# Moving expert 1's weight preparation and expert 0's scalings off VectorE, and ending the last expert on a single tile

## The chip, the cores and the metric

The kernel runs on one core of a Trainium2 chip. The time is device microseconds of one execution; the median of three executions before the change is 903.67 us (902.35 to 905.14). The core's engines are named as the profile names them: PE (TensorE, matrix products), DVE (VectorE), ACT (ScalarE), POOL (GpSimd) and SP (the queue that starts the transfers).

## The reference

An xLSTM-like recurrence (4 batches, 8 heads, 768 steps, head size 40) makes x of shape 3072 x 320. A soft mixture of 8 experts follows, and then the part that the change is about:

```
logits = x @ w_gate ; P = exp(logits - max)
for _ in range(8):
    P /= P.sum(1) + 1e-9 ; P /= P.sum(0) + 1e-9 ; P *= N / E      # Sinkhorn
for e in range(8):
    h = maximum(x @ w1[e], 0) ; out += P[:, e:e+1] * (h @ w2[e])   # F = 1024
```

N is 3072, D 320, F 1024. x here is the output of the soft mixture, of the form c @ slot_out with 32 slots, so x @ w1[e] is one product with 96 rows on the contraction side (three f16 pieces of 32).

## The kernel before

The 3072 rows are 24 tiles of 128 (`acc[:, i, :]` holds the sum of tile i, 128x320 f32). Matrix products run in f16 with each operand split in a high and a low half: h*w is hh*wh + hh*wl + hl*wh. The low half of a weight or of an activation is "value minus high half", so each split costs one cast and one subtraction.

Expert 0 is done in six blocks of four tiles (`g1`, `g2`). Its sums go to `acc` unscaled, since its combine weights are known only after the eight Sinkhorn steps, which run beside it on DVE (`sinkhorn_a`, `sinkhorn_b`, one half of a step after some of the tiles; `SK` lists them). `EXTRA` lists what else is issued after each of those tiles: the maxima of expert 1's w2 (`amax`), its scale (`pow2_w`), its high and low halves (`prep_1`), and the halves of its first-layer operand (`s1_c`). Ps[:, i, e] is the combine weight of tile i and expert e times two scales (`scale_p`, L1157 to L1161).

Experts 1 to 7 go through a planner in slots. A unit is one tile (`One`, 4 slots) or a pair of tiles (`Two`, 7 slots, a Strassen-like scheme with 7 products for 2x2 blocks). Eight triples (One, Two) make an expert: 88 slots. A unit's first-layer products and their ReLUs (`produce`: PE writes z into one of three PSUM banks, ACT and DVE read it) are issued 14 slots ahead of its second-layer products (`consume`). `Two` needs sums of quarters of w2 (`sum_w`, in place in `raw`) and their halves (`sum_h`, `sum_l`). Later expert weights are prepared by ACT and POOL (`prep_s`, `sum_l` with e other than 1) at slots fixed by `plan`. A unit's sums are added to `acc` by `drain`, `drain_x` and `drain_y`; for expert 1 each is preceded by `first` (L1553 to L1555), which multiplies the 128x320 tile of expert 0 by Ps[:, i, 0].

ACT, DVE, POOL and PE work their instructions strictly in the order of issue here (a manual schedule), so whatever stands ahead of an instruction on its engine delays it. A z bank comes free when the last ReLU that reads it is done; PE waits for it there.

Of the kernel before, what the change touches and what calls it, by code (L numbers as in the profile page):

```python
# [20 lines left out]
def mlstm_moe_kernel(  # L21
# [1459 lines left out]

    def quarter(a, b):
        return raw[:, a * KH:(a + 1) * KH, b * DH:(b + 1) * DH]

    SUMS = [((0, 0), (0, 1), (0, 0), ALU.subtract), ((0, 1), (1, 1), (0, 1), ALU.subtract),
            ((1, 1), (0, 0), (1, 1), ALU.subtract), ((1, 0), (1, 0), (1, 1), ALU.add)]

    def sum_w(j):
        o, a, b, op = SUMS[j]
        nc.gpsimd.tensor_tensor(out=quarter(*o), in0=quarter(*a), in1=quarter(*b), op=op)  # L1490

    def sum_h(e, j):
        nc.scalar.activation(
            out=wth[:, e % 2, j], in_=quarter(*SUMS[j][0]), func=AF.Copy, scale=scw[e][1] if e == 1 else 1.0,
        )
# [207 lines left out]
    for tt in range(TPB):  # L1703
        st = (NB - 2) * TPB + tt
        plan(4 * tt + 3, sinkhorn, st)
        for op, kk in EXTRA.get(st, ()):
            plan(4 * tt + 3, op, 1, kk)

    def prep_s(e, kk):
        ks = slice(2 * kk, 2 * kk + 2)  # L1710
        t = src2[e][:, ks, :]
        nc.scalar.activation(out=t, in_=t, func=AF.Copy, scale=scw[e][1])  # L1712
        nc.gpsimd.tensor_tensor(out=wl[e][:, ks, :], in0=t, in1=wh[e][:, ks, :], op=ALU.subtract)  # L1713
# [112 lines left out]
```

## Time and profile before

| | us |
|---|---|
| median of three executions | 903.67 (902.35 to 905.14) |
| the profiled execution | 898.99 |
| its span, first to last instruction | 897.3 |
| PE busy | 862.9 (96%) |
| DVE busy | 716.1 (80%) |
| ACT busy | 558.1 (62%) |
| POOL busy | 588.9 (66%) |

Busy is the time in which an engine had an instruction under way. A row of the timeline reads: start, duration, engine, line, operation, output <- input, shapes; in square brackets stands how long the engine was idle before it and what ended that. Rows with x2 or more are several instructions merged. A row of the waits reads: engine and tile that waited <- what released it: total, times, longest.

### The profile page before, as it was taken

The page shows a single profiled execution, that of the slowest core. Times are in us where ns is not written, and L with a number is a line of the kernel's source. Part 1 is how long each engine was busy: PE and PEld are TensorE (multiplying, and loading weights), DVE is VectorE, ACT ScalarE, POOL GpSimd, SP SyncE. Part 2 cuts the span into 40 slices and gives each one's busy share as a digit, 9 for nine tenths or more (in the row PEclk, how much of TensorE's full clock was granted, in tenths as well). Part 3 has the DMA queues.
Part 4 walks back from the last instruction along what each step waited for, and adds up shares of the span by engine and source line. Part 5 has one row for each costly group of instructions (what it writes and reads, how often), then busy time and mean ns, then how long its engine had stood idle before and what let it go on. Part 6 is the DMA issues. An engine that isn't in the chain of part 4 may idle for free.

```text
span 897.3 us, 26669 instructions
## 1 busy us (share of the span) xinstructions
PE 862.9 (96%) x10996; PEld 728.8 (81%) x10996; DVE 716.1 (80%) x1534; ACT 558.1 (62%) x1110; POOL 588.9 (66%) x596
## 2 busy tenths in 40 slices
PE   7999997899998989999999999999999999999997
PEld 5878884356676878888999899989889998988996
DVE  7777875455899989897788788878987897888774
ACT  7656653353245567668766776687577767767662
POOL 5766660000014679967996799689769977997663
PEclk9999999999999999999999999999999999999999
DMA  8999999960100121204110201051100110000111
GB/s 170 173 199 185 191 248 323 326 182 1 55 6 30 31 57 26 60 2 39 45 60 2 66 16 61 5 64 45 31 5 10 40 31 5 19 1 31 46 46 60
DMA packets 136402, 67.11 MB, mean 75 GB/s; under 512 B 105209, under 2 KB 130041, under 8 KB 136281
## 3 DMA queue, kind: packets, MB, share of 16 engines
q1 hardware_dynamic: 136009, 64.92, 30.1%
q8 instruction: 86, 1.41, 0.7%
q14 instruction: 35, 0.29, 0.2%
q10 hardware_dynamic: 224, 0.30, 0.1%
q0 software_dynamic: 48, 0.20, 0.1%
HBM read 60.17 MB, written 5.02 MB: 73 GB/s over the span
## 4 chain that ended last, share of the span: by engine, by line
PE 66%; DVE 10%; DMA 7%; POOL 7%; issue 5%; ACT 3%; SPq 1%; DVEq 0%; POOLq 0%; ACTq 0%
PE y L1540 15%; PE z L1508 6%; POOL op L1520 3%; DMA bigy<-in_moe_w_dram 3%; PE pss L432 2%; DVE tmr L1517 2%; PE ptk L383 2%; PE oa L477 2%; PE y L1312 2%; PE y L1313 2%; PE y L1314 2%; DMA wa<-in_moe_w_dram 1%; POOL raw L1490 1%; PE pe L402 1%; DVE acc L1560 1%
## 5 line engine op out<-in xcount | busy, mean ns | idle before, releaser
L1520 POOL TENSOR_TENSOR op<-tmr,op 128x512 f16<-128x512 f32 x280 | 319.1, 1168 | 22.1 <-ACT op L1588 19.0
L1635 PEld LDWEIGHTS <-op 128*128 128x128 f16 x4704 | 328.3, 98 | 0.6 <-issue 0.5
L1588 ACT CAST op<-tmr 128x512 f16<-128x512 f32 x280 | 170.0, 616 | 108.1 <-DVE tmr L1517 55.7
L1540 PE MATMUL y<-wx,ch 128*128 128x320 f16 x1344 | 219.0, 299 | 0.0
L1517 DVE SCALAR_TENSOR_TENSOR tmr<-z,tmr 128x512 f32<-128x512 f32 x168 | 114.7, 683 | 56.5 <-ACT op L1514 50.0
L1540 PEld LDWEIGHTS <-ch 128*128 128x128 f16 x1344 | 122.7, 98 | 35.0
L1508 PE MATMUL z<-cst,sst 96*128 96x128 f16 x1344 | 131.0, 219 | 11.7 <-DVE tmr L1517 4.9
L1594 POOL TENSOR_TENSOR tmr<-tmr 128x512 f32<-128x512 f32 x56 | 71.2, 1271 | 95.2 <-ACT tmr L1514 95.2
L1508 PEld LDWEIGHTS <-sst 96*128 96x128 f16 x1344 | 100.2, 98 | 33.6 <-issue 11.3
L1514 ACT ACTIVATE tmr<-z 128x512 f32<-128x512 f32 x112 | 64.8, 596 | 63.5 <-PE z L1508 51.7
L1517 DVE SCALAR_TENSOR_TENSOR ch<-z,ch 128x512 f16<-128x512 f32 x112 | 77.0, 688 | 18.1 <-ACT ch L1514 16.6
L1517 DVE SCALAR_TENSOR_TENSOR op<-z,op 128x512 f16<-128x512 f32 x112 | 76.2, 681 | 0.0
L1514 ACT ACTIVATE ch<-z 128x512 f16<-128x512 f32 x112 | 66.1, 591 | 2.8 <-PE my__8101 L1635 1.3
L1514 ACT ACTIVATE op<-z 128x512 f16<-128x512 f32 x112 | 66.6, 595 | 0.1
L1490 POOL TENSOR_TENSOR raw<-raw 128x640 f32<-128x640 f32 x28 | 43.8, 1565 | 8.3 <-DVE acc L1323 7.3
L1314 PE MATMUL y<-wh,hl 128*128 128x320 f16 x160 | 47.8, 299 | 0.3 <-DVE hl L1295 0.3
L1312 PE MATMUL y<-wh,hh 128*128 128x320 f16 x160 | 47.8, 299 | 0.0
L1313 PE MATMUL y<-wl,hh 128*128 128x320 f16 x160 | 47.8, 299 | 0.0
L411 ACT ACTIVATE dd<-pe 128x512 f32<-128x512 f32 x48 | 29.2, 609 | 29.4 <-PE pe L402 28.9
L1294 ACT ACTIVATE hh<-z 128x512 f16<-128x512 f32 x48 | 26.6, 595 | 33.1 <-PE z L1291 32.8
L1713 POOL TENSOR_TENSOR wx<-raw,wx 128x640 f16<-128x640 f32 x24 | 33.6, 1408 | 15.1 <-ACT raw L1712 15.1
L439 DVE TENSOR_TENSOR dd<-pss,dd 128x512 f32<-128x512 f32 x48 | 31.0, 685 | 14.7 <-PE pss L432 11.9
(1078 smaller groups left out, 1653.0 us busy)
## 6 DMA issues: line engine op xcount, KB each, us to landing
wa<-in_moe_w_dram SPq DMA_DIRECT2D x18, 512.0 KB
raw<-in_moe_w_dram SPq DMA_DIRECT2D x28, 320.0 KB
kq<-in_k_dram SPq DMA_DIRECT2D x24, 160.0 KB
kq<-in_q_dram SPq DMA_DIRECT2D x24, 160.0 KB
vz<-in_v_dram SPq DMA_DIRECT2D x24, 160.0 KB
xr<-in_o_gate_dram SPq DMA_DIRECT2D x24, 160.0 KB
wb<-in_moe_w_dram SPq DMA_DIRECT2D x6, 640.0 KB
out_dram<-acc SPq DMA_DIRECT2D x24, 160.0 KB
```

The lines of the kernel that those rows point to most:

```text
L1312: nc.tensor.matmul(y, hh[:, kc, ts], wh[e][:, kc, :], start=(kc == 0), stop=False)
L1313: nc.tensor.matmul(y, hh[:, kc, ts], wl[e][:, kc, :], start=False, stop=False)
L1314: nc.tensor.matmul(y, hl[:, kc, ts], wh[e][:, kc, :], start=False, stop=(kc == KF - 1))
L1490: nc.gpsimd.tensor_tensor(out=quarter(*o), in0=quarter(*a), in1=quarter(*b), op=op)
L1508: nc.tensor.matmul(z[:, k, :], Sst[e][:, kc * P:(kc + 1) * P], cst[:, i * P:(i + 1) * P], start=True, stop=True,)
L1514: nc.scalar.activation(out=o, in_=z, func=AF.Relu)
L1517: nc.vector.scalar_tensor_tensor(out=o, in0=z, scalar=0.0, in1=x, op0=ALU.max, op1=op)
L1520: nc.gpsimd.tensor_tensor(out=o, in0=x, in1=h, op=ALU.subtract)
L1540: nc.tensor.matmul(self.y, self.at(a, kc), b[self.e][:, kc, :], start=(kc == a == 0 and b is wh), stop=(kc == KF - 1 and a == 1),)
L1588: cast = lambda m, x: nc.scalar.copy(out=hi(m), in_=x)
L1594: at(0, lambda: nc.gpsimd.tensor_tensor(out=s1_, in0=r21, in1=r22, op=ALU.add))
L1635: nc.tensor.matmul(t[:, c * DH:(c + 1) * DH], o[:, m, a, kp, :], b[kp], start=(kp == a == 0 and b is bh), stop=(kp == KH - 1 and a == 1),)
```

## The change

- Preparation of expert 1. The low halves of its w2 (four `prep_d` on DVE, 128x640 each) become one ACT instruction that scales `raw` in place and one POOL subtraction each (`prep_s`). The four quarter sums (POOL), their casts (ACT) and low halves (DVE before, POOL now) are issued after the tiles of steps 13 to 16 of expert 0, where they stood in slots 4 to 16 of the planner. The maxima and scales come one or two tiles earlier, and the next expert's w2 is loaded from slot 4 on in place of slot 17.
- `scale_p` (8 calls) is two ACT instructions where it was one DVE instruction with two scales.
- `first` (24 calls, 128x320) moves from DVE to ACT, and is issued at the start of a One, and at slots 0 and 3 of a Two, in place of just ahead of the addition.
- In expert 7 the triples are (Two, One) in place of (One, Two), so the kernel ends on a One. At the join of experts 6 and 7 two units of kind Two follow each other.

```diff
     def scale_p(e):
-        nc.vector.tensor_scalar(
-            out=Ps[:, :, e], in0=Pm[:, :, e], scalar1=sch[e][0], scalar2=scw[e][0], op0=ALU.mult, op1=ALU.mult,
-        )
+        for t, sc in ((Pm, sch[e][0]), (Ps, scw[e][0])):
+            nc.scalar.activation(out=Ps[:, :, e], in_=t[:, :, e], func=AF.Copy, scale=sc)
...
-    def prep_1(e, kk):
-        if kk == 0:
-            pow2_w(e)
-        prep_w2(e, kk, kk + 1)
+    def prep_s(e, kk):
+        ks = slice(2 * kk, 2 * kk + 2)
+        t = src2[e][:, ks, :]
+        nc.scalar.activation(out=t, in_=t, func=AF.Copy, scale=scw[e][1])
+        nc.gpsimd.tensor_tensor(out=wl[e][:, ks, :], in0=t, in1=wh[e][:, ks, :], op=ALU.subtract)
...
-    EXTRA = {2: [(amax, 0)], 3: [(amax, 1)], 4: [(amax, 2)], 5: [(amax, 3)], 7: [(prep_1, 0)], 9: [(prep_1, 1)],
-             10: [(s1_c, 0), (s1_c, 1)], 12: [(s1_c, 2), (s1_c, 3)], 14: [(prep_1, 2)], 16: [(prep_1, 3)]}
...
+    EXTRA = {2: [(amax, 0)], 3: [(amax, 1)], 4: [(amax, 2), (amax, 3)], 6: [(pow2_w,)],
+             7: [(prep_a, 0), (prep_s, 0)], 8: [(prep_a, 1), (prep_s, 1)], 9: [(s1_c, 0), (s1_c, 1)],
+             10: [(prep_a, 2), (prep_s, 2)], 11: [(s1_c, 2), (s1_c, 3)], 12: [(prep_a, 3), (prep_s, 3)],
+             13: [(sum_w, 0), (sum_w, 1)], 14: [(sum_h, 0), (sum_h, 1), (sum_w, 2), (sum_w, 3)],
+             15: [(sum_h, 2), (sum_h, 3), (sum_l, 0), (sum_l, 1)], 16: [(sum_l, 2), (sum_l, 3)]}
...
-    def sum_l(e, j):
-        t, h, o = quarter(*SUMS[j][0]), wth[:, e % 2, j], wtl[:, e % 2, j]
-        if e == 1:
-            nc.vector.scalar_tensor_tensor(out=o, in0=t, scalar=scw[e][1], in1=h, op0=ALU.mult, op1=ALU.subtract)
-        else:
-            nc.gpsimd.tensor_tensor(out=o, in0=t, in1=h, op=ALU.subtract)
...
         def first(self, i):
-            if self.e == 1:
-                nc.vector.tensor_scalar_mul(acc[:, i, :], acc[:, i, :], Ps[:, i, 0:1])
+            a = acc[:, i, :]
+            nc.scalar.activation(out=a, in_=a, func=AF.Copy, scale=Ps[:, i, 0:1])
...
+            if e == 1 and k in (0, 3):
+                at(0, lambda: self.first(self.i if k else self.j))
...
-            units += [One(e, i, None), Two(e, i + 1, i + 2, twos)]
-            units[-2].buf = ones_
+            units += [One(e, i, ones_), Two(e, i + 1, i + 2, twos)]
+            if e == E - 1:
+                units[-2:] = [Two(e, i, i + 1, twos), One(e, i + 2, ones_)]
```

DVE at the last Sinkhorn step (Pm is P, ca the column factor, ch and op the activations of a One and a Two, wt the halves of the quarter sums), before:

```order
L1393 TENSOR_SCALAR ca<-psk 128x8
L1397 RECIPROCAL ca<-ca 128x8
L1398 TENSOR_TENSOR Pm<-Pm,ca 128x192
L1159 TENSOR_SCALAR Ps<-Pm,iv_3146,iv_2974 128x24
L1159 TENSOR_SCALAR Ps<-Pm,iv_3775,iv_3724 128x24
L1500 SCALAR_TENSOR_TENSOR wt_4093<-raw,sc_3725,wt_4092 128x640
L1574 COPY acc<-y 128x320
L1517 SCALAR_TENSOR_TENSOR tmr<-z,tmr 128x512
L1517 SCALAR_TENSOR_TENSOR op_4097<-z,op_4097 128x512
L1517 SCALAR_TENSOR_TENSOR tmr<-z,tmr 128x512
L1500 SCALAR_TENSOR_TENSOR wt_4093<-raw,sc_3725,wt_4092 128x640
L1517 SCALAR_TENSOR_TENSOR op_4097<-z,op_4097 128x512
```

The same place on DVE with the change:

```order
L1392 TENSOR_SCALAR ca<-psk 128x8
L1396 RECIPROCAL ca<-ca 128x8
L1397 TENSOR_TENSOR Pm<-Pm,ca 128x192
L1577 COPY acc<-y 128x320
L1519 SCALAR_TENSOR_TENSOR tmr<-z,tmr 128x512
L1519 SCALAR_TENSOR_TENSOR op_4113<-z,op_4113 128x512
L1519 SCALAR_TENSOR_TENSOR tmr<-z,tmr 128x512
L1519 SCALAR_TENSOR_TENSOR op_4113<-z,op_4113 128x512
```

The two Ps and the low halves of the sums no longer stand ahead of the ReLUs that free the z banks.

POOL from the last two partition maxima on (mr), before:

```order
L1113 ISA mr_3723<-mx 128x4
L1113 ISA mr_3774<-mxs 128x1
L1490 ISA
L1490 TENSOR_TENSOR raw<-raw 128x4x160 x2
L1594 TENSOR_TENSOR tmr<-tmr 128x512
L1520 TENSOR_TENSOR op_4097<-tmr,op_4097 128x512
L1490 TENSOR_TENSOR raw<-raw 128x4x160
L1520 TENSOR_TENSOR op_4097<-tmr,op_4097 128x512 x3
L1490 TENSOR_TENSOR raw<-raw 128x4x160
L1520 TENSOR_TENSOR op_4097<-tmr,op_4097 128x512
```

The same place on POOL with the change:

```order
L1113 ISA mr_3644<-mxs 128x1
L1113 ISA mr_3708<-mx 128x4
L1441 ISA
L1441 TENSOR_TENSOR wx<-raw,wx 128x640 x4
L1456 TENSOR_TENSOR raw<-raw 128x4x160 x4
L1462 TENSOR_TENSOR wt_3408<-raw,wt_3407 128x640 x4
L1597 TENSOR_TENSOR tmr<-tmr 128x512
L1522 TENSOR_TENSOR op_4113<-tmr,op_4113 128x512 x5
```

All twelve preparations of expert 1 now stand ahead of the first unit of kind Two.

POOL at the join of experts 6 and 7, before (the first tmr row belongs to the last Two of expert 6, the second to the first Two of expert 7):

```order
L1594 TENSOR_TENSOR tmr<-tmr 128x512
L1520 TENSOR_TENSOR op_4296<-tmr,op_4296 128x512 x5
L1502 TENSOR_TENSOR wt_4093<-raw,wt_4092 128x640 x2
L1594 TENSOR_TENSOR tmr<-tmr 128x512
L1520 TENSOR_TENSOR op_4097<-tmr,op_4097 128x512 x5
```

And with the change:

```order
L1597 TENSOR_TENSOR tmr<-tmr 128x512
L1522 TENSOR_TENSOR op_4307<-tmr,op_4307 128x512 x5
L1597 TENSOR_TENSOR tmr<-tmr 128x512
L1462 TENSOR_TENSOR wt_3408<-raw,wt_3407 128x640
L1522 TENSOR_TENSOR op_4113<-tmr,op_4113 128x512
L1462 TENSOR_TENSOR wt_3408<-raw,wt_3407 128x640
L1522 TENSOR_TENSOR op_4113<-tmr,op_4113 128x512 x4
```

The second Two's first addition is issued four slots earlier, ahead of expert 7's last two low halves.

## Rows read from the trace of the kernel before

**Rows 1.** Stretches: length; PE, PEld, DVE, ACT, POOL busy us; clock, DMA, GB/s
```profile
200.00:282.00 82.00, 81.72 (x619) 57.43 (x617) 65.27 (x148) 34.87 (x66) 9.14 (x9) 1.00 0.05 17
282.00:380.03 98.03, 89.08 (x1104) 78.51 (x1101) 89.92 (x170) 62.83 (x121) 77.84 (x64) 1.00 0.17 47
380.03:810.13 430.10, 426.27 (x5403) 383.49 (x5401) 360.43 (x725) 305.04 (x591) 361.46 (x301) 1.00 0.14 29
```

**Rows 2.** PE timeline, first second-layer product of experts 1, 2 and 7
```profile
286.93 0.98 PE L1540 MATMUL y<-wx,ch 128*128 128x320 f16 x6
...
380.03 0.98 PE L1540 MATMUL y<-wx,ch 128*128 128x320 f16 x6
...
810.13 0.98 PE L1540 MATMUL y<-wx,ch 128*128 128x320 f16 x6
```

**Rows 3.** Waits of PE, 282 to 380 us (total, times, longest)
```profile
PE z L1508 <- DVE tmr L1517: 3.0, 2, 2.2
PE z L1508 <- DVE ch L1517: 2.9, 4, 1.3
PE z L1508 <- ACT tmr L1514: 2.0, 1, 2.0
```

**Rows 4.** Waits of PE, 380 to 400 us and 400 to 810.2 us
```profile
PE z L1508 <- DVE ch L1517: 1.4, 2, 1.0
...
PE z L1508 <- DVE tmr L1517: 1.9, 2, 0.9
```

**Rows 5.** PE timeline, the longest of these waits
```profile
285.06 0.40 PE L1508 MATMUL z<-cst,sst 96*128 96x128 f16 x4 [2.24 <-DVE tmr L1517]
```

**Rows 6.** DVE timeline in front of that wait
```profile
277.71 0.79 DVE L1398 TENSOR_TENSOR Pm<-Pm,ca 128x192 f32<-128x192 f32 x1
278.53 2.53 DVE L1159 TENSOR_SCALAR Ps<-Pm,iv,iv 128x24 f32<-128x24 f32 x2
```

**Rows 7.** DVE groups by line, 282 to 392 us: busy, mean ns
```profile
L1555 DVE TENSOR_SCALAR acc<-acc,Ps 128x320 f32<-128x320 f32 x24 | 17.4, 726 | 0.0
...
L1500 DVE SCALAR_TENSOR_TENSOR wt<-raw,sc,wt 128x640 f16<-128x640 f32 x4 | 5.8, 1458 | 0.0
```

**Rows 8.** Lines L1159 and L1555 on DVE: ns min/median/max
```profile
L1159 DVE TENSOR_SCALAR Ps<-Pm,iv,iv x8: 991/1278/4739, 278.5 to 801.7; 128x24 f32<-128x24 f32 x8
...
L1555 DVE TENSOR_SCALAR acc<-acc,Ps x24: 374/668/1339, 294.5 to 383.9; 128x320 f32<-128x320 f32 x24
```

**Rows 9.** ACT groups of the same or the nearest shape, whole span
```profile
L170 ACT ACTIVATE xr<-xr 128x320 f32<-128x320 f32 x20 | 10.0, 498 | 0.0
...
L633 ACT ACTIVATE ct_all<-ct_all 128x128 f32<-128x128 f32 x6 | 1.9, 310 | 9.3 <-DVE ct_all L630 9.3
```

**Rows 10.** The page's groups: POOL's quarter sums and low halves
```profile
L1490 POOL TENSOR_TENSOR raw<-raw 128x640 f32<-128x640 f32 x28 | 43.8, 1565 | 8.3 <-DVE acc L1323 7.3
...
L1713 POOL TENSOR_TENSOR wx<-raw,wx 128x640 f16<-128x640 f32 x24 | 33.6, 1408 | 15.1 <-ACT raw L1712 15.1
```

**Rows 11.** DVE timeline in a Sinkhorn step
```profile
264.96 0.36 DVE L1398 TENSOR_TENSOR Pm<-Pm,ca 128x192 f32<-128x192 f32 x1
...
267.50 1.28 DVE L1295 SCALAR_TENSOR_TENSOR hl<-z,hh 128x512 f16<-128x512 f32 x2
```

**Rows 12.** POOL, ACT and PE timelines, join of experts 6 and 7
```profile
794.55 5.63 POOL L1520 TENSOR_TENSOR op<-tmr,op 128x512 f16<-128x512 f32 x5
...
800.21 1.26 ACT L1514 ACTIVATE tmr<-z 128x512 f32<-128x512 f32 x2 [1.29 <-POOL op L1520]
...
798.59 0.98 PE L1540 MATMUL y<-wx,ch 128*128 128x320 f16 x6
```

**Rows 13.** DVE timeline, the end
```profile
886.22 0.55 DVE L1560 SCALAR_TENSOR_TENSOR acc<-y,Ps,acc 128x320 f32<-128x320 f32 x1 [1.00 <-PE y L1540]
...
892.10 0.33 DVE L1663 TENSOR_TENSOR mz__14812<-my__14830,q 128x160 f32<-128x160 f32 x1 [2.05 <-PE my__14830 L1635]
...
893.28 1.01 DVE L1674 SCALAR_TENSOR_TENSOR acc<-mz__14812,Ps,acc 128x320 f32<-128x320 f32 x2
```

More of the change, by code (lines that the diff above doesn't have):

```diff
@@ L1436, in mlstm_moe_kernel, with quarter, sum_w, sum_h @@
     NBLK = E * NB
-    def prep_1(e, kk):
-        if kk == 0:
-            pow2_w(e)
-        prep_w2(e, kk, kk + 1)
-    SK = [1, 3, 5, 7, 9, 11, 13, 15, 17]
-    EXTRA = {2: [(amax, 0)], 3: [(amax, 1)], 4: [(amax, 2)], 5: [(amax, 3)], 7: [(prep_1, 0)], 9: [(prep_1, 1)],
-             10: [(s1_c, 0), (s1_c, 1)], 12: [(s1_c, 2), (s1_c, 3)], 14: [(prep_1, 2)], 16: [(prep_1, 3)]}
+    def prep_s(e, kk):
[3 more added lines that the diff above has]
+        nc.gpsimd.tensor_tensor(out=wl[e][:, ks, :], in0=t, in1=wh[e][:, ks, :], op=ALU.subtract)
+    SK = [1, 3, 5, 7, 9, 11, 13, 15, 17]
+    DH = DM // 2
+    KH = KF // 2
+    wth, wtl = (xacc.tile([P, 2, 4, KH, DH], F16, tag=f"by{j}", name=f"wt{j}") for j in (2, 3))
+    def quarter(a, b):
+        return raw[:, a * KH:(a + 1) * KH, b * DH:(b + 1) * DH]
+    SUMS = [((0, 0), (0, 1), (0, 0), ALU.subtract), ((0, 1), (1, 1), (0, 1), ALU.subtract),
+            ((1, 1), (0, 0), (1, 1), ALU.subtract), ((1, 0), (1, 0), (1, 1), ALU.add)]
+    def sum_w(e, j):
+        o, a, b, op = SUMS[j]
+        nc.gpsimd.tensor_tensor(out=quarter(*o), in0=quarter(*a), in1=quarter(*b), op=op)
+    def sum_h(e, j):
+        nc.scalar.copy(out=wth[:, e % 2, j], in_=quarter(*SUMS[j][0]))
+    def sum_l(e, j):
+        nc.gpsimd.tensor_tensor(
+            out=wtl[:, e % 2, j], in0=quarter(*SUMS[j][0]), in1=wth[:, e % 2, j], op=ALU.subtract,
+        )
+    EXTRA = {2: [(amax, 0)], 3: [(amax, 1)], 4: [(amax, 2), (amax, 3)], 6: [(pow2_w,)],
[3 more added lines that the diff above has]
+             15: [(sum_h, 2), (sum_h, 3), (sum_l, 0), (sum_l, 1)], 16: [(sum_l, 2), (sum_l, 3)]}
+    def extra(st):
+        for op, *kk in EXTRA.get(st, ()):
+            op(1, *kk)
     def sinkhorn(st):
@@ L1464, in mlstm_moe_kernel @@
             g2(n, tt)
-            if n == 3 and tt == 0:
+            if n == 2 and tt == 1:
                 s1_p(1)
@@ L1472, in mlstm_moe_kernel @@
             sinkhorn(st)
-            for op, kk in EXTRA.get(st, ()):
-                op(1, kk)
-    wth, wtl = (xacc.tile([P, 2, 4, KH, DH], F16, tag=f"by{j}", name=f"wt{j}") for j in (2, 3))
+            extra(st)
     op_a = ctx.enter_context(tc.tile_pool(name="op_a", bufs=1, side="right", reuse_waits="tile"))
@@ L1480, in mlstm_moe_kernel @@
     chl = [op_a.tile([P, 2, KF, P], F16, name=f"ch{j}") for j in range(2)]
[L1482 to L1495, printed above, removed]
-    def sum_l(e, j):
-        t, h, o = quarter(*SUMS[j][0]), wth[:, e % 2, j], wtl[:, e % 2, j]
-        if e == 1:
-            nc.vector.scalar_tensor_tensor(out=o, in0=t, scalar=scw[e][1], in1=h, op0=ALU.mult, op1=ALU.subtract)
-        else:
-            nc.gpsimd.tensor_tensor(out=o, in0=t, in1=h, op=ALU.subtract)
     def z_(e, i, hf):
@@ L1525, in __init__ @@
         def __init__(self, e, i, buf):
-            self.e, self.i, self.h = e, i, chl[buf % 3] if buf is not None else None
+            self.e, self.i, self.buf = e, i, buf
         def produce(self, k, at):
@@ L1536, in consume @@
                 self.y = psy.tile([P, TB], F32, tag="y", name="y")[:, 0:DM]
+                if self.e == 1:
+                    at(0, lambda: self.first(self.i))
             w = KF // self.slots
@@ L1705, in mlstm_moe_kernel @@
         plan(4 * tt + 3, sinkhorn, st)
[L1706 to L1713, printed above, removed]
+        plan(4 * tt + 3, extra, st)
     def plan_sums(c, e, sums, his, los):
         for j in range(4):
-            plan(c + sums[j], sum_w, j)
+            plan(c + sums[j], sum_w, e, j)
             plan(c + his[j], sum_h, e, j)
             plan(c + los[j], sum_l, e, j)
-    plan_sums(4, 1, (0, 3, 6, 9), (2, 5, 8, 11), (3, 6, 9, 12))
     def s1_v():
@@ L1749, in steps @@
             plan(c + d, f)
+    plan(4, load_w2, 2)
     for e in range(1, E - 1):
```

7 lines of the change are left out of this document (1 added, 6 removed).

## The prediction

> **What bounds the kernel now.** I read the busy shares first, then three long stretches, then what PE waits for in each, then the engine that it waits for. PE is busy for 96% of the span, so time can only come from where PE stands still or starts late. In 200 to 282 us (expert 0 with the Sinkhorn steps) PE is busy for 81.7 of 82 us: no instruction taken from another engine can make this stretch shorter, though POOL works for only 9.1 us there [rows 1]. In 282 to 380 us, expert 1, PE has 89.1 of 98, while DVE has 89.9, more than PE itself. In 380 to 810, experts 2 to 6, PE has 426.3 of 430 and DVE 84% [rows 1]. So DVE bounds expert 1, and PE everything around it. The starts of the experts say the same: expert 1 takes 380.03 - 286.93 = 93.1 us, experts 2 to 6 take (810.13 - 380.03) / 5 = 86.0 each with the same PE work [rows 2]. The waits show how: PE waits for a z bank that a DVE ReLU (tmr, ch) still reads, 5.9 us in all, and once 2.0 for an ACT one [rows 3].
>
> **The change part by part.** Terms are against the profiled execution, 898.99 us, whose span is 897.3.
>
> *Before expert 1.* The longest wait, 2.24 us at 285.06 [rows 5], stands behind two Ps (2.53 us together) on DVE [rows 6], and then the first low half of a quarter sum. All leave DVE's queue there. What is late next: ACT now holds four Ps instructions ahead of the second tmr ReLU; the nearest shape takes 0.31 [rows 9], so 1.2 us after Pm is final (278.5 [rows 6]), and that ReLU ends near 280.3 (its own 0.6). Its bank is asked for at the slot before the one that waits, after 281. I take -2.0; ends -2.2 and -1.0.
>
> *Expert 1.* DVE loses 24 scalings, 17.4 us, and four low halves, 5.8 us [rows 7]; 89.9 - 23.2 leaves 66.7 of 98, a smaller share than the 84% at which experts 2 to 6 run. ACT gains 24 scalings at 0.498, the same shape [rows 9]: 12.0 us on top of 62.8 of 98 [rows 1], less two of the casts that move out ahead. Its total, some 75%, is near the 71% of experts 2 to 6 (305.0 of 430.1). The scalings are issued three to four slots before the addition that needs them, so DVE doesn't wait for them. Expert 1 should then run like its successors: 93.1 - 86.0 = 7.1, and I take -7.0 because ACT's weight preparation already cost PE its one ACT wait [rows 3]. Ends: -7.7 if it also loses the waits that experts 2 to 6 still have (3.3 us over five, [rows 4]), and -3.7 if only the DVE waits inside it go (5.9 - 2.2).
>
> *Start of expert 2.* Two waits for ch, 1.4 us [rows 4], come while DVE still works off expert 1's last additions; experts 3 to 6, with the same instructions at the same slots, have none of these. I take -1.2; ends -1.4 and 0.
>
> *Ps of experts 4 to 7.* L1159 takes 1.28 us as a rule and 4.74 at most, the last one at 801.7 [rows 8]; the two waits for tmr in 400 to 810 (1.9 us, [rows 4]) lie behind the two long ones. On ACT it is two short instructions. I take -1.8; ends -1.9 and -0.9 (half).
>
> *Sinkhorn steps.* Twelve POOL instructions move in: four at 1.408, four at 1.565 [rows 10], and four low halves taken at 1.408, 17.5 us; the last eight, 11.9 us, follow one another about 262 to 275 us. The other additions there are ACT's, which has 34.9 of 82 busy [rows 1]. But some DVE instructions run longer beside POOL: Pm times ca takes 0.36 with POOL idle [rows 11] and 0.79 beside it [rows 6]; a scaling of 128x320 takes 0.374 at best, 0.726 on average and 1.339 at worst [rows 7, 8]. Each step has three such instructions (two products of Pm, one sum with 1e-9), and two steps lie in POOL's unbroken stretch: six times 0.43 (the same instruction's own difference) is 2.6 us on DVE, six times 0.97 is 5.8. The ReLUs that free the z banks stand behind them (1.28 us at 267.50, [rows 11]). Expert 1's low halves no longer stand in these steps, which pays for about 1.1 of it. I take +1.5; ends 0 and +5.8.
>
> The Trainium skill, SBUF — State Buffer, section "Who interferes with whom", says that a DVE instruction with two SBUF inputs, or in a two-port mode, and a POOL instruction shut each other out for whole instructions. It speaks against putting POOL work beside the Sinkhorn steps, and for taking the scalings off DVE. The 0.374 to 1.339 us agree with it (a wait of up to one POOL instruction); the 4.74 us do not, being longer than one. By the rule alone a wait ends with the POOL instruction under way, which stays within the 5.8 above.
>
> *Join of experts 6 and 7.* The second Two starts four slots sooner, and its first ReLU writes a tmr that the first Two's last POOL subtraction still reads. That subtraction ends at 794.55 + 5.63 = 800.2, and ACT already waited 1.29 us for it [rows 12]. With the change ACT stands there earlier, but the ReLU can't end before 800.8. PE wants that bank for its fourth z at the One that begins at 798.59 [rows 12], say 798.8. So +2.0; ends 0 (the earlier relief moves POOL forward) and +4.0 (the next bank waits for POOL's addition too).
>
> *End.* After PE's last product DVE works from 892.10 to 893.28 + 1.01 = 894.3, 2.2 us; a One ends with one addition of 0.55 [rows 13]. That is -1.6, with nothing hiding it on either side; one transfer less at the end is counted at nothing, since the last of them is as late as its addition.
>
> Earlier loads of the next expert's w2 and the moved s1_p cost nothing: the maxima that need the load are 17 slots behind it, and PE's work is the same in another order.
>
> Sum: -2.0 - 7.0 - 1.2 - 1.8 + 1.5 + 2.0 - 1.6 = -10.1, so 888.9 for the profiled execution. The three executions' median stands 4.7 higher than the profiled one, and I keep that: 903.67 - 10.1 = 893.6.
>
> **The rivals.** *DVE shut out in the Sinkhorn steps.* Two of eight L1159 took 4.7 us [rows 8] where the median is 1.28. If two of the six instructions beside POOL's stretch fare so, DVE loses 2 x 4.4 = 8.8 and PE that much in place of 1.5: -10.1 + 7.3 = -2.8, 900.9. For it: POOL works without a gap there. Against it: the only Pm product seen beside POOL lost 0.43.
>
> *ACT takes DVE's place in expert 1.* ACT works in order, and each scaling stands ahead of ReLUs that free z banks. If the 24 scalings and the first four Ps fall on PE's path whole, they cost 12.0 + 1.2 = 13.2 us: -10.1 + 13.2 = +3.1, 906.8, slower than before. It decides from 10.1 of the 13.2 us on. At half of it the time is 900.2. For it: ACT already held PE up once for 2.0 us [rows 3]. Against it: ACT is idle for 35 of 98 us in expert 1 [rows 1].
>
> *More than the sum.* All terms at their better end, with no cost in the steps and at the join: -2.2 - 7.7 - 1.4 - 1.9 - 1.6 = -14.8, 888.9.
>
> **How the numbers follow.** The forecast with its own spread has 0.68 (about 890 to 898), the better end 0.04, DVE shut out 0.13, ACT at half 0.10, ACT whole 0.05. The range is 888.5 to 901: the better end and the two cases near 900 are in, ACT whole and the far half of the others are out. A measurement of this kernel tells 0.3% from no change, 2.7 us: faster means below 901.0, slower above 906.4. Faster: 0.68 + 0.04 + 0.6 of 0.23 = 0.86; slower: 0.03 of ACT whole and 0.01 of unforeseen waits = 0.04; the same: the remaining 0.10.
>
> **What would show it.** Expert 1's starts 86 us apart, no 2.2 us wait ahead of it, no DVE L1159 and no ch wait at expert 2's start; one new wait of about 2 us of PE behind a tmr at the join; a last DVE addition of 0.55. PE below 80 of 82 us in the Sinkhorn stretch, behind Pm products longer than 1 us, would mean the first rival; waits of PE for ACT in expert 1 the second. Wrong altogether would be an expert 1 that still takes over 90 us with DVE idle.

## The result, and the profile after

The changed kernel takes 893.57 us in the median (890.33 to 895.74), the kernel before on the same chip 904.23 (902.35 to 905.14): a ratio of 0.9882 (95% interval 0.9847 to 0.9917). The forecast was 893.6. The median agrees with it; the sum behind it does not. By the traces the terms come to less than half of what I forecast, and the rest is made up by something that no trace shows, as told below.

The profiled execution takes 893.87 us, its span is 892.1. The three stretches, cut where those of [rows 1] are, the last two at the first products of experts 2 and 7 (length; PE, PEld, DVE, ACT, POOL busy us; clock, DMA share, GB/s):

```profile
200.00:282.00 82.00, 79.17 (x595) 55.27 (x594) 64.29 (x142) 37.46 (x72) 18.32 (x15) 1.00 0.11 33
282.00:372.97 90.97, 90.56 (x1123) 80.33 (x1122) 70.36 (x145) 74.51 (x152) 77.54 (x65) 1.00 0.17 36
372.97:801.30 428.33, 426.10 (x5412) 384.16 (x5410) 347.97 (x715) 308.36 (x603) 361.54 (x302) 1.00 0.14 29
```

In expert 1 PE now lacks 0.4 us of 91 where it lacked 9 of 98, and DVE has fallen from 92% to 77%. In the Sinkhorn stretch PE lacks 2.8 of 82, where it lacked 0.3. The first second-layer products of experts 1, 2 and 7 (PE's timeline; expert 7 now begins with a Two, so its first row reads mx), against [rows 2]:

```profile
287.26 0.98 PE L1544 MATMUL y<-wx,ch 128*128 128x320 f16 x6
...
372.97 0.98 PE L1544 MATMUL y<-wx,ch 128*128 128x320 f16 x6
...
801.30 1.00 PE L1638 MATMUL mx__13502<-wx,op 128*128 128x160 f16 x12
```

Expert 1 takes 85.7 us in place of 93.1. What PE waits for, from 230 to 282 us and from 380 to the end (total, times, longest), against [rows 3, 4]:

```profile
PE z L1290 <- DVE hl L1294: 2.4, 2, 1.6
PE z L1510 <- DVE ch L1519: 0.4, 1, 0.4
...
PE mz__13553 L1638 <- DVE acc L1679: 2.9, 1, 2.9
PE z L1510 <- ACT tmr L1516: 1.8, 1, 1.8
PE z L1510 <- DVE ch L1519: 0.4, 1, 0.4
```

A Two has three PSUM sums; mz is the one that its fourth slot begins. All waits of [rows 3] but a 0.4 are gone, and so are those of [rows 4] and the 2.24 us of [rows 5]. In their place stand two groups. The first is in the Sinkhorn steps. DVE's timeline (what answers to the 0.36 of [rows 11]) and POOL's:

```profile
257.53 0.18 DVE L1383 TENSOR_SCALAR rw<-rw 128x24 f32<-128x24 f32 x1
...
265.26 1.04 DVE L1397 TENSOR_TENSOR Pm<-Pm,ca 128x192 f32<-128x192 f32 x1
...
266.72 1.02 DVE L1383 TENSOR_SCALAR rw<-rw 128x24 f32<-128x24 f32 x1
...
268.11 1.43 DVE L1385 TENSOR_TENSOR Pm<-Pm,rw 128x192 f32<-128x192 f32 x1
...
273.61 1.63 DVE L1397 TENSOR_TENSOR Pm<-Pm,ca 128x192 f32<-128x192 f32 x1
...
275.65 0.87 DVE L1383 TENSOR_SCALAR rw<-rw 128x24 f32<-128x24 f32 x1
```

```profile
263.19 1.40 POOL L1441 TENSOR_TENSOR wx<-raw,wx 128x640 f16<-128x640 f32 x1 [7.11 <-ACT raw L1440]
264.54 6.40 POOL L1456 TENSOR_TENSOR raw<-raw 128x640 f32<-128x640 f32 x4
270.90 5.59 POOL L1462 TENSOR_TENSOR wt<-raw,wt 128x640 f16<-128x640 f32 x4
```

The three products of Pm that start between 263 and 274 us take three to four and a half times their 0.36, the two sums in L1383 five to six times the 0.18 of an earlier step; the ReLUs (hl) behind them come late. The second group is the join of experts 6 and 7: PE's timeline, then four windows of 2 us after the wait (the clock stands behind POOL's busy time):

```profile
790.01 0.38 PE L1510 MATMUL z<-cst,sst 96*128 96x128 f16 x4 [1.83 <-ACT tmr L1516]
...
801.08 0.38 PE L1510 MATMUL z<-cst,sst 96*128 96x128 f16 x4
...
806.89 1.78 PE L1638 MATMUL mz__13553<-wt,op 128*128 128x160 f16 x12 [2.94 <-DVE acc L1679]
```

```profile
806.00:808.00 2.00, 1.11 (x9) 1.11 (x10) 2.00 (x5) 0.00 (x0) 1.62 (x2) 0.53 0.00 0
808.00:810.00 2.00, 2.00 (x19) 2.00 (x17) 1.27 (x5) 1.41 (x3) 1.16 (x1) 0.50 0.00 0
810.00:812.00 2.00, 2.00 (x19) 2.00 (x17) 0.67 (x2) 0.60 (x1) 0.00 (x0) 0.50 0.00 0
812.00:814.00 2.00, 2.00 (x22) 1.89 (x21) 0.73 (x2) 0.00 (x0) 0.00 (x0) 0.77 0.00 0
```

Behind a standstill of 2.94 us PE works from 806.1 to 812.9 us at the lower of its two levels (0.50 of 2.4 GHz), and twelve products take 1.78 us where they take 0.99 at full clock (in the run with the early drain, below). The work that went to ACT, as its groups by line from 284 to 376 us and over the whole span, against [rows 7 to 9]:

```profile
L1559 ACT ACTIVATE acc<-acc,Ps 128x320 f32<-128x320 f32 x24 | 13.3, 556 | 0.0
...
L1160 ACT ACTIVATE Ps<-Ps,iv 128x24 f32<-128x24 f32 x8 | 2.7, 339 | 0.3
```

A scaling takes 0.556 where I took 0.498, a Ps 0.34 where I took 0.31. At the end one addition is left, against the three of [rows 13]:

```profile
888.72 0.55 DVE L1563 SCALAR_TENSOR_TENSOR acc<-y,Ps,acc 128x320 f32<-128x320 f32 x1 [0.99 <-PE y L1544]
```

**The lengths that the experiments are read by.** Five stretches of each kernel's trace: A from ACT's first cast in step 4 (226.05 us before, 225.70 now; what the change moves comes behind it) to expert 1's first second-layer product, B expert 1, C experts 2 to 6, D expert 7 up to PE's last product, E from there to the end of the span. Then A to E together against the kernel before, and the ratio of medians on one chip with its interval. E goes by the span, which is listed to 0.1 us.

| kernel | A | B | C | D | E | all | ratio |
|---|---|---|---|---|---|---|---|
| before | 60.88 | 93.10 | 430.10 | 81.86 | 5.31 | | |
| changed | 61.56 | 85.71 | 428.33 | 87.38 | 3.42 | -4.8 | 0.9882 (0.9847 to 0.9917) |
| changed, again | 61.55 | 85.71 | 428.35 | 85.95 | 3.46 | -6.2 | 0.9896 (0.9864 to 0.9928) |
| old order | 61.54 | 85.71 | 425.26 | 81.86 | 5.30 | -11.6 | 0.9845 (0.9816 to 0.9874) |
| last triple | 61.55 | 85.70 | 425.27 | 82.52 | 3.48 | -12.7 | 0.9838 (0.9810 to 0.9867) |
| no low halves | 61.56 | 85.71 | 428.30 | 85.74 | 3.44 | -6.5 | 0.9890 (0.9857 to 0.9923) |
| shorter lead | 61.54 | 85.72 | 427.25 | 86.15 | 3.41 | -7.2 | 0.9869 (0.9836 to 0.9903) |
| early drain | 61.53 | 85.71 | 428.37 | 81.40 | 3.41 | -10.8 | 0.9867 (0.9840 to 0.9894) |
| first alone | 61.95 | 86.44 | 429.87 | 81.85 | 5.25 | -5.9 | 0.9920 (0.9893 to 0.9947) |
| preparation alone | 61.58 | 90.86 | 431.68 | 81.86 | 5.26 | 0.0 | 0.9966 (0.9946 to 0.9986) |
| scale_p alone | 58.68 | 96.08 | 425.27 | 81.85 | 5.28 | -4.1 | 0.9932 (0.9905 to 0.9959) |
| ACT doubled | 61.56 | 90.16 | 428.33 | 86.13 | 3.44 | -1.6 | 0.9956 (0.9936 to 0.9977) |
| POOL held back | 63.26 | 85.68 | 429.20 | 85.06 | 3.43 | -4.6 | 0.9897 (0.9867 to 0.9927) |
| best | 59.34 | 85.69 | 425.03 | 82.50 | 3.50 | -15.2 | 0.9816 (0.9787 to 0.9844) |

C and D of two kernels with different orders in expert 7 are compared only as a sum. Where all eight triples are reversed, two groups of four first-layer products (z) come to stand ahead of expert 7's first second-layer product: 1088 products of PE in expert 6's stretch and 1016 in expert 7's, in place of 1080 and 1024. A group takes 0.22 us (801.08 to 801.30 above), so 0.44 us of work moves from D to C.

A stretch with the same instructions comes again to within 0.05 us in most cases (0.24 at most, C of the best kernel) unless the clock falls in it, so 1 us is read from one trace here, while medians need many runs: the cast of step 4 alone, with the same program ahead of it, starts between 222.15 and 227.83 us in these traces. By the medians every kernel gains more on the kernel before than by this table (0.4 to 2.5 us more in two of the four comparisons on one chip, 3 to 6 in the other two); the section on the prediction comes back to that.

### The profile page after: what moved, and what is told of

Same layout as the page of the kernel before. It is cut to its first block, busy times and chain, and to the rows that moved or that the text cites. A ratio compares the mean times of both kernels' runs of the same rounds, so it can differ in the third digit from the quotient of the medians.

```text
span 892.1 us, 26688 instructions
## 1 busy us (share of the span) xinstructions
PE 866.0 (97%) x10996; PEld 732.4 (82%) x10996; DVE 683.0 (77%) x1494; ACT 574.6 (64%) x1154; POOL 596.3 (67%) x604
## 4 chain that ended last, share of the span: by engine, by line
PE 83%; DVE 5%; DMA 4%; POOL 3%; ACT 3%; issue 1%; SPq 1%; POOLq 0%; ACTq 0%; DVEq 0%
PE y L1544 19%; PE z L1510 8%; PE pss L432 3%; PE ptk L383 2%; PE oa L477 2%; POOL op L1522 2%; PE y L1311 2%; PE y L1312 2%; PE y L1313 2%; PE pe L402 1%; PE ob L488 1%; DMA wb<-in_moe_w_dram 1%; DMA wa<-in_moe_w_dram 1%; PE pu L1016 1%; DMA bigy<-in_moe_w_dram 1%
## 5 line engine op out<-in xcount | busy, mean ns | idle before, releaser
L1441 POOL TENSOR_TENSOR wx<-raw,wx 128x640 f16<-128x640 f32 x28 | 39.1, 1405 | 39.4 <-ACT raw L1440 39.4
L439 DVE TENSOR_TENSOR dd<-pss,dd 128x512 f32<-128x512 f32 x48 | 30.9, 685 | 15.2 <-PE pss L432 12.4
```

## The experiments

**The changed kernel once more**, and **the old order** in expert 7:

```diff
-            if e == E - 1:
-                units[-2:] = [Two(e, i, i + 1, twos), One(e, i + 2, ones_)]
```

> The changed kernel as it is, once more, so that it stands against the other kernels of this round on one chip, and to see whether the join's waits and the lower clock after them are in every execution. My theory: the waits (1.83, 0.40, 2.94 us near 790 to 807 us) come from the order of instructions and come again to within 0.1 us; the granted clock falls behind the 2.94 us standstill again; expert 7 to PE's last product about 87 us, and a ratio to before of about 0.993 (-6 us by the markers of the trace, against the -10.7 of the first medians). Rival: the clock drop was a chance, expert 7 takes about 84 us and the ratio is near 0.989.

> The changed kernel with expert 7's triples back in the order (One, Two), all else kept. My theory: in the trace of the changed kernel the join of experts 6 and 7 costs about 7.5 us (waits of 1.83, 0.40 and 2.94 us and then some 6 us at granted clock 0.5), against 1.7 us won at the end; so 893.6 - 7.5 + 1.7 = 887.8 us, expert 7's first product to PE's last back from 87.2 to about 82, no PE wait over 1 us between 785 and 815 us, granted clock 1.00 there. Rival: the lower clock in that one trace has nothing to do with the order, and the join costs the 2.0 us of the prediction: 893.6 - 2.0 + 1.6 = 893.2 us, with a clock below 1 again somewhere in expert 7.

The waits of 1.83, 0.40 and 2.94 us came again to within 0.01 us, and so did the lower clock, for a shorter time (807.7 to 811.1 us; D 85.95). With the old order all three are gone, C is 3.1 us shorter and D 4.1 to 5.5, and the clock stays at 1.00 there; the end costs its 1.9 us again. So the order costs 7.2 to 8.6 us at the join; the rival's 2 us is wrong. The ratio of the repeated run, 0.9896, stands at the rival's 0.989, and its interval ends just short of the 0.993 of my theory; D lies between the two forecasts. So the waits come every time, while what the clock adds to them differs.

**Only the last triple reversed**, so that the two Twos meet near the end.

```diff
-            if e == E - 1:
+            if e == E - 1 and i == NT - 3:
```

> The changed kernel with only the last triple of expert 7 reversed: two units of kind Two follow each other near the end in place of at the join, where POOL has no quarter sums of the next expert to make. My theory: the join's price is due to POOL's low halves standing in front of the second Two's subtractions; here the two Twos cost 0 to 2 us (ACT still waits for POOL's last subtraction, as 1.64 us in the trace of the changed kernel), and the end keeps its 1.7 us: 886 to 888 us, say 887. Rival: two Twos in a row cost the same wherever they stand (the second one's third group needs the PSUM bank that the first one's last addition still reads): 893.6 us, with a PE wait of 2 to 3 us near 875 to 885 us.

885.08 us against 898.97, just below the forecast 886 to 888, on a chip where the kernel before is faster too. D is 82.52, 0.7 us for the two adjacent Twos, inside the forecast 0 to 2, and E keeps its gain. The longest wait of PE there:

```profile
871.21 0.99 PE L1638 MATMUL mx__14753<-wx,op 128*128 128x160 f16 x12 [0.23 <-DVE acc L1563]
```

For mz it waits 0.1 us. The reason that I gave for this, POOL's low halves, did not survive the next two runs. What differs here in DVE's order is that no ReLU of a later Two stands ahead of the first Two's closing additions, since none is left to do.

**Without the last two low halves**, and **a shorter lead** for expert 7's first Two:

```diff
-            plan(c + los[j], sum_l, e, j)
+            if e < E - 1 or j < 2:
+                plan(c + los[j], sum_l, e, j)
```
```diff
-            zat.setdefault(max(c - LEAD[type(u)] + k, 0), []).append((u, k))
+            zat.setdefault(max(c - (10 if u.e == E - 1 and u.i == 0 else LEAD[type(u)]) + k, 0), []).append((u, k))
```

> The changed kernel without the last two low halves (sum_l 2 and 3) of expert 7's quarter sums; the products read what expert 5 left there, so the small correction that they carry is left out for expert 7. On POOL 2.8 us go from between the two adjacent Twos. My theory: the first wait of 1.83 us stays (it stands ahead of them), the second chain (POOL 2.8 us late, ACT 1.64, DVE 2.49, PE 2.94) goes, and with it the lower clock: expert 7 takes 82 to 83 us and the kernel gains 5 us on the changed one. Rival: the 2.94 us wait is the price of the PSUM bank with two Twos adjacent and stays above 2 us without them: gain below 2 us.

> The changed kernel with the first-layer products of expert 7's first Two issued 10 slots ahead in place of 14, so that they stand 11 slots behind those of the Two before it, as everywhere else. My theory: the join's price comes from ReLUs that are issued four slots too early, and so stand on ACT in front of work that could go on while they wait for POOL; with 10 slots PE's waits between 785 and 815 us are below 1 us in all, the clock stays up, expert 7 takes about 82 to 83 us: 8 us faster than the changed kernel. Rival: two Twos in a row at that place cost a wait anyway, by POOL's two low halves in between or by the second Two's PSUM bank: waits of 2 us or more remain, and the gain is below 4 us.

Both missed, and both times the rival's PSUM bank is what came. PE without the low halves:

```profile
786.51 0.38 PE L1510 MATMUL z<-cst,sst 96*128 96x128 f16 x4 [1.87 <-ACT tmr L1516]
...
802.91 1.68 PE L1638 MATMUL mz__13551<-wt,op 128*128 128x160 f16 x12 [2.54 <-DVE acc L1679]
```

POOL's 2.8 us were worth 0.4 of the 2.94. With the shorter lead the first wait is 1.34 in place of 1.83 + 0.40, and the second stays whole:

```profile
803.24 1.66 PE L1638 MATMUL mz__13553<-wt,op 128*128 128x160 f16 x12 [2.94 <-DVE acc L1679]
```

So the 2.94 us are not POOL's low halves', but for 0.4, nor the early ReLUs'. What is left is DVE's own order. Without the low halves it runs, ahead of that wait:

```profile
798.87 0.69 DVE L1519 SCALAR_TENSOR_TENSOR tmr<-z,tmr 128x512 f32<-128x512 f32 x1 [2.02 <-ACT op L1516]
799.48 0.68 DVE L1519 SCALAR_TENSOR_TENSOR op<-z,op 128x512 f16<-128x512 f32 x1
800.07 0.68 DVE L1519 SCALAR_TENSOR_TENSOR tmr<-z,tmr 128x512 f32<-128x512 f32 x1
800.67 0.32 DVE L1668 TENSOR_TENSOR mz__13414<-my__13437,q 128x160 f32<-128x160 f32 x1
...
801.85 1.01 DVE L1679 SCALAR_TENSOR_TENSOR acc<-mz__13414,Ps,acc 128x320 f32<-128x320 f32 x2
```

The five closing additions of the first Two (from 800.67) stand behind three ReLUs of the next Two but one, which themselves wait 2.02 us for ACT, and free the bank at 802.86. The mx and mz of the Twos take turns in two PSUM banks, so the mz of two Twos in a row share one; the second Two asks for it three slots after the first one's last product. With a One between them it is seven.

**Early drain.** The test of that:

```diff
-                at(1, self.drain_y)
+                if e == E - 2 and self.j == NT - 1:
+                    at(0, self.drain_y, True)
+                else:
+                    at(1, self.drain_y)
```

> The changed kernel with the five closing additions of expert 6's last Two (drain_y) issued on DVE ahead of the three ReLUs that stand before them, a slot earlier; nothing else moves. My theory, the third on the join: the second Two asks for the PSUM bank of mz three slots after the first Two's last product, and with a One between them it would be seven; the additions that free it stand on DVE behind ReLUs of the next unit but one, so 2.94 us are waited and the granted clock falls. Ahead of them they are done before the bank is asked for: the wait for mz falls below 0.5 us, the clock stays at 1.00 there, expert 7 takes 82 to 83.5 us in place of 86 to 87.4, and the kernel gains 3 to 5 us on the changed one; the first wait (1.8 us, behind POOL) stays. Rival: the ReLUs held back make PE wait for their z banks instead: a new wait of 2 us or more for z at the same place, gain below 2 us.

DVE, then PE, at the same place:

```profile
798.57 0.33 DVE L1671 TENSOR_TENSOR mz__13416<-my__13439,q 128x160 f32<-128x160 f32 x1 [0.92 <-ACT mz__13416 L1649]
...
799.75 1.01 DVE L1682 SCALAR_TENSOR_TENSOR acc<-mz__13416,Ps,acc 128x320 f32<-128x320 f32 x2
800.68 0.68 DVE L1519 SCALAR_TENSOR_TENSOR tmr<-z,tmr 128x512 f32<-128x512 f32 x1
```

```profile
801.08 0.99 PE L1638 MATMUL mz__13553<-wt,op 128*128 128x160 f16 x12
```

The wait is gone, no new one came, the clock stays at 1.00, and D falls from 86 or more to 81.40, a gain of 4.6 to 6.0 us where 3 to 5 were forecast. C stays at 428.37, so the first wait (1.87 and 0.40 us here) is another's: by the trace it is ACT's, which waits for POOL's last reading of tmr; no run removed this one alone. By C and D together the join is then two costs. With the early drain they are 509.77 against 507.12 in the old order, so 2.65 us belong to the first wait. The changed kernel's two traces have 515.71 and 514.30, so 4.5 to 5.9 us belong to DVE's late additions, of which 2.94 is the wait and the rest the clock and what follows.

**One part alone.** `first` on ACT alone, the preparation in the Sinkhorn steps alone, and `scale_p` on ACT alone; each is the part of the change of that name, put on the kernel before (the second by putting all the others back, so that the new EXTRA, prep_s and sums are what is left).

```diff
-                nc.vector.tensor_scalar_mul(acc[:, i, :], acc[:, i, :], Ps[:, i, 0:1])
+            nc.scalar.activation(out=a, in_=a, func=AF.Copy, scale=Ps[:, i, 0:1])
...
-        nc.vector.tensor_scalar(
-            out=Ps[:, :, e], in0=Pm[:, :, e], scalar1=sch[e][0], scalar2=scw[e][0], op0=ALU.mult, op1=ALU.mult,
+        for t, sc in ((Pm, sch[e][0]), (Ps, scw[e][0])):
+            nc.scalar.activation(out=Ps[:, :, e], in_=t[:, :, e], func=AF.Copy, scale=sc)
```

> The kernel before with only the 24 scalings of expert 0's sums moved to ACT, issued ahead as in the change. My theory: these 17.4 us are three quarters of what leaves DVE, and the rest of expert 1 then has room: expert 1 takes about 87 us in place of 93.1, the ch waits at expert 2's start go (1.2): 904.2 - 6.1 - 1.2 = 897 us. Rival: ACT still has the casts of the quarter sums there and takes DVE's place: PE waits for ACT in expert 1 for over 3 us in all, and the time is 900 us or more.

> The changed kernel with the scalings of expert 0 (first), the combine weights (scale_p) and the order of expert 7 as before, so that only expert 1's preparation has moved to POOL and ACT in the Sinkhorn steps. My theory: the steps lose 2.8 us (Pm and rw of 0.9 to 1.6 us on DVE beside POOL's unbroken stretch), the wait of 2.24 us ahead of expert 1 shrinks to about 1 (two combine weights still there, the low half gone), expert 1 gains about 1.5: 904.2 + 2.8 - 1.2 - 1.5 = 904.3 us, no change. Rival: the steps' loss is made up by the low halves that left them (0.8 us or less in all): 902 us or below, with PE waits of less than 1 us between 255 and 280 us.

> The kernel before with the combine weights alone (scale_p, 8 calls) as two ACT instructions each. My prediction took 1.8 us for experts 4 to 7 and put the 2.24 us ahead of expert 1 down to these and a low half together. My theory now, from the kernels with parts of the change: experts 2 to 6 take 425.3 us where all parts but the order are in, 429.9 with the scalings alone: so the Ps on DVE cost some 4 us there, expert 7's first product comes 3 to 4.5 us sooner, the wait ahead of expert 1 falls below 1.5 us, and the kernel gains 4 to 5.5 us. Rival, the prediction's size: 1.8 us in experts 2 to 6, a gain of 3 us or less.

By stretches the parts give -5.9, 0.0 and -4.1 us, together -10.0; the kernel with all three and the old order has -11.6. But the clock fell once in `first` alone (286.2 to 289.7 us) and once in `scale_p` alone (331.2 to 334.6 us). Half of each stretch, an estimate of 1.7 us, was lost by that; without it the parts come to some -13.4, more than the whole. Three readings lie in that:

- The 2.24 us of [rows 5] needed both the two Ps and the low half on DVE: with either one moved, no wait of that size is left, though the preparation takes POOL's sums away from there as well (A falls by 2.2 with `scale_p` alone; with the preparation alone nothing over 0.4 us is waited there, and A is longer only for the new 2.4 us in the Sinkhorn steps).
- Experts 2 to 6 reach their full gain, 4.8 us, with `scale_p` alone: 425.27, against 429.9 and 431.7 without it. Not all of it needs `scale_p`. Some 2.0 of the 4.8 stand at expert 2's start, and `first` alone takes them away too: there PE waits nowhere between 367 and 503 us. What it still has is a wait of 0.3 at 503 us and the waits behind three Ps of 4.7 us, where the kernel before has two and the preparation alone has four.
- `scale_p` alone makes expert 1 3.0 us longer, 96.08. A start that comes earlier is waited for again in a stretch that DVE bounds; the longest waits are these:

```profile
PE z L1507 <- ACT tmr L1513: 3.5, 2, 2.0
PE z L1507 <- DVE ch L1516: 1.8, 3, 1.0
PE z L1507 <- DVE tmr L1516: 1.3, 1, 1.3
```

  But that is only some 1.3 us of the 3.0. The other 1.7 are the clock, which fell behind the 2.0 us wait for ACT, while the kernel before kept it behind the same wait ([rows 3]). The window 332 to 334 us, first with `scale_p` alone, then before:

```profile
332.00:334.00 2.00, 2.00 (x18) 2.00 (x16) 2.00 (x4) 1.99 (x4) 2.00 (x3) 0.50 0.07 10
...
332.00:334.00 2.00, 2.00 (x33) 2.00 (x31) 2.00 (x4) 2.00 (x5) 2.00 (x3) 1.00 0.06 4
```

With `first` alone the wait of [rows 5] is there as before, 2.23 us, but this time the clock fell behind it (PE, and the windows as above):

```profile
285.53 0.40 PE L1508 MATMUL z<-cst,sst 96*128 96x128 f16 x4 [2.23 <-DVE tmr L1517]
```
```profile
286.00:288.00 2.00, 2.00 (x11) 1.14 (x10) 2.00 (x4) 0.85 (x2) 1.96 (x3) 0.56 0.08 11
288.00:290.00 2.00, 2.00 (x12) 1.23 (x10) 2.00 (x4) 1.92 (x4) 2.00 (x2) 0.59 0.91 295
```

A is 1.1 us longer than before for that alone. The preparation alone is worth nothing by the trace, as expected (+0.7, -2.2 and +1.6 in A, B and C), with the expected waits of 0.8 and 1.6 us in the Sinkhorn steps; by the medians it gains 2.5 us (896.44 against 898.97), which is the rival's size. `first` alone gains 6.3 us by the medians (892.69), where 7.3 were forecast, and expert 1 takes 86.4 of the forecast 87. `scale_p` alone gains 6.5 by the medians (892.88), above the forecast 4 to 5.5, and 4.1 by the trace; expert 7 starts 4.5 us sooner, as forecast.

**ACT doubled.** Each `first` is followed by one more scaling into a spare tile.

```diff
+            nc.scalar.activation(out=ot.tile([P, DM], F32, tag="spare", name="spare", bufs=1), in_=a, func=AF.Copy, scale=Ps[:, i, 0:1])
```

> The changed kernel with each of expert 1's 24 scalings on ACT followed by one more of the same shape into a spare tile: some 13 us more on ACT between expert 1's and expert 2's first products. My theory: ACT had room, since PE waits for it nowhere in expert 1: at most 2 us longer than the 85.7 between the two first products. Rival (the prediction's: ACT takes DVE's place): ACT is near the edge and PE takes half of the added work or more: 92 us or more, with PE waits for ACT of over 3 us.

Between the two: expert 1 takes 90.16, 4.5 us more, for 24 x 0.562 = 13.5 us of added work. The waits in it:

```profile
PE z L1510 <- DVE ch L1519: 2.7, 3, 1.0
PE z L1510 <- ACT tmr L1516: 1.2, 2, 0.8
```

The change's own 24 scalings fit, the next 24 do so for two thirds. The prediction's ACT rival was wrong here, but by a nearer miss than I thought.

**POOL held back.** A tiny POOL copy of cl ahead of each group of preparations makes the group start only after DVE's products of Pm:

```diff
+    def pool_after(e):
+        nc.gpsimd.tensor_copy(out=seen, in_=cl)
...
+             7: [(pool_after,), (prep_a, 0), (prep_s, 0), (prep_a, 1), (prep_s, 1)],
+             9: [(pool_after,), (s1_c, 0), (s1_c, 1), (prep_a, 2), (prep_s, 2), (prep_a, 3), (prep_s, 3)],
...
+             13: [(pool_after,), (sum_w, 3), (sum_l, 0), (sum_l, 1)], 14: [(sum_h, 2)],
+             15: [(pool_after,), (sum_h, 3), (sum_l, 2), (sum_l, 3)]}
```

> The changed kernel with one tiny POOL copy of cl (the last thing that a Sinkhorn half step writes on DVE) ahead of each group of two or three of POOL's twelve preparations, so that POOL starts a group only when DVE has left its products of Pm; the groups stand after steps 7, 9, 11, 13 and 15. My theory: Pm and rw took 0.9 to 1.6 us beside POOL's unbroken stretch because POOL shut them out; now Pm takes 0.36 and rw 0.18 in nearly all steps, the PE waits of 2.84 us between 255 and 280 us fall below 0.5, and the way from the ACT cast of step 7 to expert 1's first product shrinks from 48.80 to 46.2 to 46.6 us: 2.4 us faster than the changed kernel. Rival: the waits come from ACT's and DVE's order of work in these steps, not from POOL: the way stays within 0.5 us of 48.8.

All Pm take 0.36 and all rw 0.18 now, so POOL was their cause. But the way from the cast of step 7, the measure of the expectation, grew from 48.80 to 50.50 us, and the kernel gained nothing on the changed one (0.9897 against 0.9896). Four ACT instructions at step 9 (two casts and two scalings of w2) stood in front of the cast that a ReLU needs, and the clock fell behind that wait too:

```profile
253.94 0.56 PE L1290 MATMUL z<-cst,sst 96*128 96x512 f16 x1 [3.19 <-DVE hl L1294]
```

**A better version**: the last triple alone reversed, and POOL held back with ACT's scalings spread over steps 7 to 10.

```diff
+             7: [(pool_after,), (prep_a, 0), (prep_s, 0)], 8: [(prep_a, 1), (prep_s, 1)],
+             9: [(pool_after,), (prep_a, 2), (prep_s, 2), (s1_c, 0), (s1_c, 1)], 10: [(prep_a, 3), (prep_s, 3)],
```

> Towards a better version: the changed kernel with only the last triple of expert 7 reversed, and POOL's groups held behind DVE's Sinkhorn products as in the kernel with the copy of cl, but with ACT's four scalings of w2 on four different tiles (steps 7 to 10), since two at once behind the first-layer operand made ACT late by 3.2 us there. My theory: Pm at 0.36 and rw at 0.18 with no wait above 0.5 us between 235 and 285 us, 46.2 to 46.8 us from the ACT cast of step 7 to expert 1's first product, no join: 0.9765 to 0.983 of before (2.4 us less than with the last triple alone, which stood at 0.9838). Rival: ACT stays late by the scalings wherever they stand: a wait of over 1.5 us remains, and the ratio is that of the last triple alone.

882.52 us against 899.34, a ratio of 0.9816 (0.9787 to 0.9844). The way from the cast of step 7 is 46.58, and A 2.2 us less than in the changed kernel, as forecast. One Pm of 0.84 and one wait (0.88, where none above 0.5 was forecast) are left:

```profile
270.27 0.84 DVE L1397 TENSOR_TENSOR Pm<-Pm,ca 128x192 f32<-128x192 f32 x1
```

## Why the prediction was right, and where it was not

By its terms, measured as differences of the stretches:

- *Before expert 1*, -2.0 and +1.5, together -0.5; measured +0.7. The first is confirmed (-2.2 with `scale_p` alone), so the Sinkhorn steps cost 2.9. The mechanism and its place were right, the size was half: five instructions between 263 and 277 us were 0.68 to 1.27 us longer than 0.36 or 0.18, where I took 0.43 for each of six; holding POOL back won 2.2 of it again. The Trainium skill (SBUF — State Buffer, "Who interferes with whom") says that a DVE instruction with two SBUF inputs contends with a POOL instruction that reads SBUF, and that the port pair which they share is an exclusive lock. The products of Pm agree: their longest excess, 1.63 - 0.36 = 1.27, is below one POOL instruction of 1.40 to 1.54.
- *The 4.74 us of [rows 8]* I put aside as longer than one POOL instruction. The trace of the kernel before shows them end with a whole run of POOL (DVE, then POOL):

```profile
801.66 4.73 DVE L1159 TENSOR_SCALAR Ps<-Pm,iv,iv 128x24 f32<-128x24 f32 x1
```
```profile
804.08 2.27 POOL L1520 TENSOR_TENSOR op<-tmr,op 128x512 f16<-128x512 f32 x2
807.72 2.36 POOL L1520 TENSOR_TENSOR op<-tmr,op 128x512 f16<-128x512 f32 x2 [1.37 <-ACT op L1588]
```

  The Ps ends at 806.39, POOL at 806.35, after four instructions without a gap that overlap the Ps. All nine Ps of this length, in the three traces that have the Ps on DVE, end 0.04 to 0.05 us after such a run. So a wait for POOL can last several of its instructions. That POOL is the cause is read from this; no run held POOL back from the Ps.
- *Expert 1*, -7.0; measured -7.39. DVE was the bound there.
- *Start of expert 2 and the Ps*, -1.2 and -1.8; measured -4.84. The mechanism was right, the size was not. I added up the 3.3 us of [rows 4]; the trace has two more waits there, 0.42 at 510.72 and 0.12 at 395.41, and each of the six delays the next start by some 0.16 us more than its listed length. That is 2.0 at expert 2's start and 2.8 behind it.
- *The join*, +2.0 with an end at +4.0; measured +8.6, and +7.2 in the second trace. This is the step that failed. The mechanism that I named (ReLU behind POOL's last reading of tmr) is there and costs some 2.6, near the 2.0. The PSUM bank of mz, 4.5 to 5.9 us, is missing from the prediction: I looked at who frees the z banks of the second Two and not at its sums' bank, which in the new order is asked for four slots sooner. And I gave a standstill no price beyond its own length; behind this one the clock fell.
- *End*, -1.6; measured -1.89.

The terms sum to -4.8 by the traces, where I had -10.1. That the median came out at 893.6 all the same is luck. I carried over the 4.7 us by which the kernel before's median lies above its profiled execution, and the changed kernel has no such distance (893.57 against 893.87 profiled, and 891.75 against 893.63 the second time). The kernel before does not always have it either: in the three later comparisons its median is 898.97, 901.24 and 899.34, 0.0 to 2.2 above the 898.99. What its other executions lose, its one trace does not show, and it stays open. Two candidates are in the traces: a clock that falls behind the 2.24 us wait, as with `first` alone, an estimate of 1.7 us; and more Ps of 4.7 us than the two of this trace (three and four in the two other traces with the Ps on DVE), each followed by a wait of PE of 0.9 to 1.8 us.

Of the rivals, DVE shut out in the Sinkhorn steps was a true mechanism at a third of the price (2.9, not 8.8). The sign that I had given for it came, PE at 79.2 of 82 us behind products of Pm longer than 1 us, so that sign did not tell the two prices apart; ACT in DVE's place was not seen; "more than the sum", -14.8, was not seen in the changed kernel (-4.8); the last triple alone comes near it with -12.7, and the best version passes it with -15.2.

## What to carry to other kernels

When units are put in another order, go through every buffer that two neighbours share, PSUM banks of the sums among them, and count for each the slots between the last reader's place in its engine's queue and the next writer. Parts of a change do not add up: a wait with two sufficient causes goes with either, and time gained ahead of a stretch with another bound is waited again in it. Where one trace's stretches repeat to 0.05 us, read the change from them, but look first where the granted clock fell in each, put the same work between the marks, and do not carry a single trace's distance to the median over to another kernel.

## What was not expected of the hardware

After standstills of PE of 2.94, 2.54 and 3.19 us the granted clock stood at 0.5 for some 3 to 7 us, and so it did once each after 2.23 and 2.05 us. After the 2.24 us of [rows 5] and the 2.0 us for ACT of [rows 3] it stayed at 1.00, and so it did after the 1.87 us that are left at the join with the early drain. With POOL held back it fell behind a wait of almost the same length at the same place:

```profile
788.78 0.38 PE L1517 MATMUL z<-cst,sst 96*128 96x128 f16 x4 [1.89 <-ACT tmr L1523]
```
```profile
790.00:792.00 2.00, 2.00 (x9) 1.19 (x8) 1.45 (x3) 1.57 (x4) 2.00 (x2) 0.50 0.05 12
```

So the length of the standstill alone does not tell, in these traces, whether the clock falls behind one of about 2 us. In two traces of the same kernel the same 2.94 us cost 5.9 and 4.5 us in all.
